# A reordered opening, weight-major FFN for the first batch, and moved masks in a fused attention and FFN kernel

## The chip, the core and the metric

The kernel runs on one core of one Trainium2 chip. The core has five engines that run side by side, each with its own instruction queue that it works through in order: TensorE (PE in the profile, matrix products), VectorE (DVE), ScalarE (ACT, which has the exponential), GpSimd (POOL) and SyncE (SP, which only issues transfers here). Sixteen DMA engines move data between the chip's main memory and the core's own memory. Matrix products land in a small accumulator memory, PSUM. An engine waits for another through semaphores.

The metric is the device time of one execution in microseconds (us), as the median of five runs.

## What is computed

There are 4 batches, 8 heads, 768 positions and 64 numbers per head. Some heads look at the whole past, the others only at the first 4 positions and the last 64. Behind the attention stands a feed-forward network (FFN) with three weights whose products are combined by maximum.

```python
scores = scale * np.matmul(q, k.transpose(0, 1, 3, 2))
causal = rel >= 0
stream_keep = causal & (is_sink | in_win)
mask = np.where(retr[0, :, 0, 0, None, None], full_mask, stream_mask)
...
a = np.exp(scores)
a = a / (np.sum(a, axis=-1, keepdims=True) + 1e-09)
return np.matmul(a, v)
...
h = np.maximum(np.maximum(x @ w1, x @ w2), x @ w3)
return h @ w_out
```

Inputs and output are 32-bit floats; the kernel computes in 16-bit floats with 32-bit sums.

## The kernel before

**Tiling.** Work is cut into steps `t` of one batch `b`, one half of the 768 positions as queries and one quad of four heads; sixteen steps, t = 0 to 15, with t = 0 and 1 the first half of batch 0, t = 2 and 3 its second half, t = 4 to 7 batch 1. A step has two pairs of heads, `i` = 0 and 1, and its scores come in units `u`: two for a first half, four for a second.

**A step.** `scores` (line 439) makes one unit's products of keys and queries in PSUM; ACT takes the exponential into `pt` (line 450). For t = 0 and 1 the mask is added inside PSUM by a product with `ident` (line 423), which needs the mask tile `mk` of those heads; for later steps the exponential is multiplied by the mask (line 477), on POOL unless `(t, i, u)` stands in `MASK_ON_DVE`. `prep_v` casts the values into `va` (line 390) and makes `vf` (line 392), which is zero for far keys in heads that don't look far. `av` (line 493) multiplies `pt` with `va` and `vf`; DVE divides by the sum (lines 501 and 503) into `x`. The transposed `x`, `xT`, is made by a DMA transpose for most steps, and by PE with a copy (lines 525 and 529, `turn_x`) for t = 0, 1 and 3.

**FFN.** When the second quad of a half is done, `ffn(b, half)` is put in a queue. It is a generator of 24 pieces: 18 groups of four products (line 336), one for each of three weights and six column blocks, and then three output rows of six products (line 362), counted as two pieces each. The group of the first weight is cast to `acc` by ACT (line 344); those of the other two are combined by maximum on DVE (line 347), the last into `hT`. `fill(n)` takes n pieces from the queue. A group holds one of four PSUM banks until its cast or maximum is done. The groups go column block by column block, three weights each, except for the first FFN, where all of the first weight comes first.

**Order.** The order on every engine is the order of the program text; nothing is rearranged. The opening, from line 537 to 592, is written out by hand. From then on `PROGRAM` (line 600) has one row for each unit of scores from t = 2: how many FFN pieces belong to it, whether its two pairs are to be apart, and four lines of other work that go between the scores and the fills: `v` (prep_v with its engines, as d, a, p), `av`, `x` (turn_x), `turn` (a DVE transpose of keys or queries, line 188), `pair` (turn_pair), `cast`, `load`, `load_v` and `gate`, which makes SP wait for an exponential before it loads further values.

**Keys and queries.** Those of batch 0 are loaded as 32-bit floats in pairs of heads (`load_pairs`), cast to 16 bits (`cast_pair`, line 137), transposed by PE and copied out as `KQ` (`turn_pair`, lines 155 and 160). In the opening, pairs 0 to 3 of the first half come by SP's and ACT's queues. Later ones, and the four weights (`load_weight`, lines 305 and 310), are issued from POOL's queue.

**Flags.** `read_flags` reads which heads look far, `head_flags` spreads this over the partitions by a product, `head_masks` makes the mask tile of two heads (line 293), and `far_flags` makes the tile `far` on DVE and copies it into `vf` on POOL (line 288). `idle_work` issues products that nobody reads.

Of the kernel before, what the change touches and what calls it, by code (L numbers as in the profile page):

```python
# [49 lines left out]
def kernel(  # L50
# [14 lines left out]
    nc = tc.nc  # L65
# [50 lines left out]
    cast = {}  # L116
# [151 lines left out]
    def read_flags():  # L268
        nc.vector.tensor_scalar(
            out=RT1, in0=ir32[:, 0 : 2 * H : 2], scalar1=0.0, scalar2=None,  # L270
            op0=ALU.not_equal,
        )

    def head_flags():
        flags = bank([P, H], FP32, "flags")
        nc.tensor.matmul(flags, base[0:1, 0:P], RT1, start=True, stop=True)
        nc.vector.tensor_copy(out=RT, in_=flags)
        nc.vector.tensor_scalar(
            out=least, in0=RT, scalar1=-1.0, scalar2=1.5, op0=ALU.mult, op1=ALU.add
        )  # L280
# [36 lines left out]
    def ffn(b, half):  # L317
        last = b == B - 1 and half == 1
        n_yy = 0

        def psum():
            nonlocal n_yy
            n_yy += 1
            if last and n_yy % 2:
                return sps.tile([P, 2, 512], FP32, tag="st", name="yst")[:, 0, :]
            return bank([P, 512], FP32, "yy")

        hT = [htp.tile([P, HALF], FP16, tag=f"hT{n}", name=f"hT{n}") for n in range(NNB)]
        acc = {}
        order = [(wi, ni) for ni in range(NNB) for wi in range(3)]  # L330
        if (b, half) == (0, 0):
            order.sort()
        for wi, ni in order:
            yy = psum()
            for ks in range(KS):
                nc.tensor.matmul(  # L336
                    yy[:, 0:HALF],
                    w_t[wi][:, ks, ni * P : (ni + 1) * P],
                    xT[b, half][ks].rearrange("p a t -> p (a t)"),
                    start=(ks == 0), stop=(ks == KS - 1),  # L340
                )
            if wi == 0:
                acc[ni] = accp.tile([P, HALF], FP16, tag="acc", name="acc")
                nc.scalar.copy(out=acc[ni], in_=yy[:, 0:HALF])  # L344
            else:
                dst = acc[ni] if wi == 1 else hT[ni]
                nc.vector.tensor_tensor(  # L347
                    out=dst, in0=yy[:, 0:HALF], in1=acc[ni], op=ALU.max
                )
            yield  # L350
        for tb in range(HB):

            parts = 2 if last and tb == HB - 1 else 1
            n = DMdl // parts
            r0 = b * S + half * HALF + tb * P
            ot = fwork.tile([P, DMdl], FP32, tag="ot", name="ot")
            for c, op, eng in (
                (0, nc.scalar.copy, nc.sync), (n, nc.vector.tensor_copy, nc.scalar),
            )[:parts]:
                yo = psum()  # L360
                for ns in range(NNB):
                    nc.tensor.matmul(  # L362
                        yo[:, 0:n],
                        hT[ns][:, tb * P : (tb + 1) * P],
                        woutt[:, ns, c : c + n],
                        start=(ns == 0), stop=(ns == NNB - 1),
                    )
                op(out=ot[:, c : c + n], in_=yo[:, 0:n])  # L368
                eng.dma_start(out=out[r0 : r0 + P, c : c + n], in_=ot[:, c : c + n])
            yield  # L370
            yield
# [83 lines left out]
                masks(t, i, u)  # L455


    MASK_ON_DVE = ((3, 1, 3), (6, 0, 1), (7, 0, 1))

    def masks(t, i, u):  # L460
        b, half, qd = where(t)
# [56 lines left out]
    def turn_x(t, i, op=None):  # L518
# [17 lines left out]
    dve, act, pool = nc.vector.tensor_copy, nc.scalar.copy, nc.gpsimd.tensor_copy  # L536
    idle_work(8)
    cast_pair(0, 0, (act, act))
    read_flags()
    head_flags()  # L540
    head_masks(0, True)
    turn_pair(0, 0, dve, dve)
    idle_work(2)
    cast_pair(0, 1, (pool, act))
    head_masks(1, True)
    turn_pair(0, 1, dve)
    cast_pair(0, 2, (pool, pool))
    scores(0, 0, (0,))
    turn_pair(0, 2, dve)
    scores(0, 0, (1,))  # L550
    head_masks(2, True)
    head_masks(3, True)
    cast_pair(0, 3, (pool, pool))
    scores(0, 1, (0,))
    load_weight(0)
    turn_pair(0, 3, dve)
    far_flags()
    prep_v(0, 0, dve, nc.gpsimd)
    scores(0, 1, (1,))
    prep_v(0, 1, dve, nc.vector)  # L560
    prep_v(1, 0, dve, nc.vector)
    scores(1, 0, (0,))
    scores(1, 1, (0,))
    prep_v(1, 1, dve, nc.gpsimd)
    load_pairs(1, 0, 2, (nc.gpsimd, nc.gpsimd))
    scores(1, 0, (1,))
    scores(1, 1, (1,))
    av(0, 0)
    load_weight(1)
    av(0, 1)  # L570
    load_pairs(1, 2, 2, (nc.gpsimd, nc.gpsimd))
    av(1, 0)
    turn_x(0, 0, act)
    turn_x(0, 1, act)
    av(1, 1)
    turn_x(1, 0, act)
    load_weight(2)
    load_v(0, 1, (nc.gpsimd,) * HB)
    load_weight(3)
    turn_x(1, 1, dve)  # L580
    cast_pair(1, 0, (dve, act))
    cast_pair(1, 1, (dve, act))
    fill(4)
    turn_pair(1, 0, dve)
    turn_pair(1, 1, dve)
    head_masks(0)
    head_masks(1)
    fill(1)
    head_masks(2)
    fill(1)  # L590
    fill(1)
    head_masks(3)

# [2 lines left out]

    FIRST = 4
    PROGRAM = (  # L600
        (2.4, True, "", "", "cast 1 2 dd", "cast 1 3 ap"),
        (2.4, False, "load 1 0", "", "", ""),
        (2.0, False, "pair 1 2", "", "", "pair 1 3"),
        (2.2, False, "load 1 1", "", "", ""),
        (2.2, True, "", "", "v 2 0 dd", "gate"),
        (1.6, True, "v 2 1 ap, load_v 1 0", "", "av 2 0", ""),
        (1.6, True, "", "x 2 0, turn 1 0 0 0, turn 1 0 0 1", "av 2 1, turn 1 0 1 1", "v 3 0 pp"),
        (3.0, False, "turn 1 0 1 0, load_v 1 1", "x 2 1", "", "v 3 1 ap"),
        (3.6, False, "", "turn 1 1 0 0, turn 1 1 0 1, turn 1 1 1 1, av 3 0", "", "v 4 0 pd"),
        (3.0, False, "av 3 1", "", "", "turn 1 1 1 0, v 4 1 ad"),  # L610
        (3.6, False, "x 3 0, x 3 1", "", "av 4 0", ""),
        (3.6, False, "", "v 5 0 ad, x 4 0, av 4 1", "", "v 5 1 ap, load 2 0"),
        (2.8, False, "", "x 4 1", "", ""),
        (3.6, False, "av 5 0, av 5 1, load 2 1", "x 5 0", "", ""),
        (3.8, False, "v 6 0 pp", "x 5 1", "", "load_v 2 0"),
        (3.4, False, "", "v 6 1 dp", "", "turn 2 0 1 0"),
        (4.8, False, "", "turn 2 0 0 1", "av 6 0", "turn 2 0 0 0"),
        (4.0, False, "", "", "x 6 0, turn 2 0 1 1", "x 6 1"),
        (3.4, False, "", "av 6 1", "turn 2 1 0 0, turn 2 1 0 1", "load_v 2 1"),
        (5.0, False, "", "v 7 0 dp", "turn 2 1 1 0, turn 2 1 1 1", ""),  # L620
        (4.0, False, "v 7 1 dp", "", "", "v 8 0 ap"),
        (3.6, False, "av 7 0, x 7 0, av 7 1", "", "", "v 8 1 dp"),
        (4.0, False, "", "v 9 0 dp", "av 8 0, x 7 1", ""),
        (4.0, False, "", "av 8 1", "x 8 0", "load 3 0"),
        (4.0, False, "", "x 8 1", "av 9 0, v 9 1 dp", ""),
        (4.0, False, "load 3 1", "", "x 9 0", ""),
        (4.2, False, "v 10 0 dp, av 9 1", "", "x 9 1", "load_v 3 0"),
        (4.0, False, "v 10 1 dp", "", "", "turn 3 0 1 0"),
        (4.0, False, "", "turn 3 0 0 1, av 10 0", "", "x 10 0, turn 3 0 0 0"),
        (4.0, False, "", "", "av 10 1, turn 3 0 1 1", ""),  # L630
        (4.4, False, "", "x 10 1", "turn 3 1 0 0, turn 3 1 0 1", "v 11 0 dp, load_v 3 1"),
        (3.2, False, "", "", "turn 3 1 1 0, turn 3 1 1 1", "v 11 1 dp"),
        (4.0, False, "", "", "av 11 0", "v 12 0 dp"),
        (4.2, False, "x 11 0, av 11 1", "", "", "v 12 1 dp"),
        (4.8, False, "", "v 13 0 dp, x 11 1", "av 12 0", ""),
        (4.0, False, "", "av 12 1", "x 12 0", ""),
        (3.2, False, "", "x 12 1", "av 13 0, v 13 1 dp", ""),
        (4.0, False, "", "", "x 13 0", ""),
        (4.0, False, "v 14 0 dp, av 13 1", "", "x 13 1", ""),
        (4.0, False, "v 14 1 dp", "", "", ""),  # L640
        (4.0, False, "", "av 14 0", "", "x 14 0"),
        (4.0, False, "", "", "av 14 1", ""),
        (4.0, False, "", "x 14 1", "", "v 15 0 pp"),
        (4.2, False, "", "", "", "v 15 1 dp"),
        (4.0, False, "", "", "av 15 0", ""),
        (4.0, False, "x 15 0, av 15 1", "", "", ""),
        (4.0, False, "", "x 15 1", "", ""),
    )
    ops = {"d": dve, "a": act, "p": pool}
    engines = {"d": nc.vector, "p": nc.gpsimd}  # L650
# [2 lines left out]
        av=lambda *a: av(*map(int, a)),  # L653
# [71 lines left out]
```

## Time and profile before

| what | value |
| --- | --- |
| median of 5 runs | 203.6 us (203.57 to 203.91) |
| the profiled execution, device time | 204.2 us |
| its span in the trace | 202.2 us |
| PE busy | 190.0 us, 94% of the span |
| DVE busy | 130.2 us, 64% |
| POOL busy | 125.5 us, 62% |
| ACT busy | 124.8 us, 62% |
| granted PE clock, mean | 0.997 |
| transfers | 26.48 MB, mean 131 GB/s |

The span runs from the first to the last instruction that the trace shows; the device time includes what lies around it. All times inside the trace count from the span's start. A row of the profile that names a group, such as `L336 PE MATMUL yy<-xT,w1t`, gives the line, the engine, the operation, and what it writes and reads. The idle time of an engine is put down to the one that it waited for last. The DMA share is the busy share of the sixteen DMA engines, and can pass 1 when their packets overlap.

### The profile page before, as it was taken

What the parts mean: (1) busy time and instruction counts of PE and PEld (TensorE: products, weight loads), DVE (VectorE), ACT (ScalarE), POOL (GpSimd) and SP (SyncE); (2) the same over time, 40 slices, a digit from 0 to 9 for tenths busy, and PEclk for the clock granted to TensorE, in tenths of its full rate; (3) what the DMA queues carried; (4) which work ended last, traced back from release to release, by engine and by line L of the source; (5) the groups of instructions that cost most, each with busy time, mean ns of one, the idle gap of its engine ahead of it and who ended that gap; (6) DMA issues with size and microseconds to landing.
All of it is one profiled execution on the core that took longest, in us unless ns stands there. A gap on an engine that the chain in (4) does not pass through costs nothing.

```text
span 202.2 us, 5148 instructions
## 1 busy us (share of the span) xinstructions
PE 190.0 (94%) x2059; PEld 108.6 (54%) x2059; DVE 130.2 (64%) x260; ACT 124.8 (62%) x188; POOL 125.5 (62%) x151
## 2 busy tenths in 40 slices
PE   7897599996799999999999999999999999999992
PEld 2454355545456456565556466574565565655552
DVE  2995698689666766985565748986647244633540
ACT  4493687887577778565758596656586776323221
POOL 3659349879996933859987906798929636700000
PEclk9999999999999999999999999999999999999998
DMA  6999999996938996532449983613301230014004
GB/s 187 267 153 225 250 246 211 214 217 144 216 102 141 198 211 138 122 56 74 145 78 204 181 199 87 138 21 124 93 19 24 83 95 19 3 41 154 3 0 156
DMA packets 43245, 26.48 MB, mean 131 GB/s; under 512 B 33558, under 2 KB 38230, under 8 KB 43222
## 3 DMA queue, kind: packets, MB, share of 16 engines
q1 hardware_dynamic: 37206, 15.01, 32.4%
q0 software_dynamic: 4784, 10.23, 26.1%
q10 hardware_dynamic: 1232, 0.92, 1.5%
q8 instruction: 16, 0.26, 0.6%
q14 instruction: 7, 0.06, 0.1%
HBM read 25.17 MB, written 6.29 MB: 156 GB/s over the span
## 4 chain that ended last, share of the span: by engine, by line
PE 78%; POOL 6%; DMA 6%; DVE 5%; ACT 2%; issue 2%; DVEq 0%; ACTq 0%
PE yy L336 41%; PE yy L362 13%; PE st L439 9%; PE oacc L493 9%; DMA w1t<-in_moe_w_dram 5%; POOL pt L477 4%; PE yst L336 3%; PE st L226 2%; DVE KQ L160 2%; DVE mk L293 1%; POOL vf L392 1%; ACT pt L450 1%; DMA out_dram<-ot 1%; PE yst L362 1%; ACT ot L368 1%
## 5 line engine op out<-in xcount | busy, mean ns | idle before, releaser
L477 POOL TENSOR_TENSOR pt<-pt,mk 128x512 f16<-128x512 f16 (+1 forms) x81 | 86.6, 1093 | 31.4 <-ACT pt L450 31.4
L450 ACT ACTIVATE pt<-st 128x1024 f16<-128x1024 f32 (+3 forms) x99 | 83.0, 894 | 26.3 <-PE st L439 25.5
L347 DVE TENSOR_TENSOR acc<-yy,acc 128x384 f16<-128x384 f32 x45 | 25.1, 559 | 25.8 <-PE yy L336 17.9
L336 PE MATMUL yy<-xT,w1t 128*128 128x384 f16 x180 | 36.5, 327 | 0.4 <-DMA w1t<-in_moe_w_dram 0.4
L336 PE MATMUL yy<-xT,w2t 128*128 128x384 f16 x180 | 36.3, 327 | 0.0
L336 PE MATMUL yy<-xT,w0t 128*128 128x384 f16 x180 | 36.1, 326 | 0.1
L344 ACT CAST acc<-yy 128x384 f16<-128x384 f32 x45 | 21.3, 481 | 19.9 <-PE yy L336 14.9
L362 PE MATMUL yy<-woutt,hT 128*128 128x512 f16 (+1 forms) x138 | 32.3, 375 | 0.0
L439 PE MATMUL st<-KQ 32*128 32x384 f16 (+5 forms) x560 | 28.5, 279 | 1.9 <-DVE KQ L188 1.2
L347 DVE TENSOR_TENSOR hT<-yy,acc 128x384 f16<-128x384 f32 x45 | 25.1, 557 | 6.4 <-PE yy L336 3.2
L493 PEld LDWEIGHTS <-pt 128*128 128x128 f16 x672 | 23.8, 97 | 5.3 <-issue 1.4
L188 DVE STREAM_TRANSPOSE KQ<-kq 128x384 f32<-128x384 f32 x24 | 25.2, 1137 | 1.0 <-DMA kq<-in_k_dram 1.0
L493 PE MATMUL oacc<-va,pt 128*128 128x65 f16 x352 | 24.8, 193 | 0.7 <-POOL pt L477 0.6
L336 PEld LDWEIGHTS <-w2t 128*128 128x128 f16 x192 | 17.6, 98 | 13.0 <-issue 1.9
L336 PEld LDWEIGHTS <-w0t 128*128 128x128 f16 x192 | 17.8, 97 | 12.2 <-issue 0.9
L336 PEld LDWEIGHTS <-w1t 128*128 128x128 f16 x192 | 17.3, 98 | 12.8 <-issue 1.0
L439 PEld LDWEIGHTS <-KQ 32*128 32x128 f16 (+1 forms) x560 | 12.2, 93 | 20.1 <-issue 13.1
L368 ACT COPY ot<-yy 128x512 f32<-128x512 f32 x22 | 12.9, 588 | 14.9 <-PE yy L362 10.7
L362 PEld LDWEIGHTS <-hT 128*128 128x128 f16 x150 | 13.9, 98 | 15.1 <-DVE hT L347 0.9
L493 PE MATMUL oacc<-vf,pt 128*128 128x65 f16 x320 | 21.3, 193 | 0.2 <-DVE vf L392 0.2
L503 DVE TENSOR_TENSOR x<-oacc,rc 128x384 f16<-128x384 f32 x32 | 17.8, 558 | 1.1
L501 DVE RECIPROCAL rc<-oacc 128x6 f32<-128x6 f32 x32 | 6.2, 193 | 18.6 <-PE oacc L493 18.3
(71 smaller groups left out, 125.3 us busy)
## 6 DMA issues: line engine op xcount, KB each, us to landing
out_dram<-ot SPq DMA_DIRECT2D x23, 256.0 KB, 2.7
vs<-in_v_dram SPq DMA_DIRECT2D x21, 256.0 KB, 5.3
kq<-in_k_dram POOLq DMA_DIRECT2D x6, 384.0 KB, 7.9
kq<-in_q_dram POOLq DMA_DIRECT2D x6, 384.0 KB, 9.5
qs<-in_q_dram ACTq DMA_DIRECT2D x4, 192.0 KB, 4.0
ks<-in_k_dram SPq DMA_DIRECT2D x4, 192.0 KB, 3.9
w0t<-in_moe_w_dram POOLq DMA_DIRECT2D x1, 768.0 KB, 7.1
ks<-in_k_dram POOLq DMA_DIRECT2D x2, 384.0 KB, 8.1
```

Of the source, the lines that this page charges most:

```text
L188: nc.vector.transpose(out=dst.rearrange("c (p j) -> c j p", j=n)[:, j0:j1], in_=src.rearrange("c (j i) -> c j i", i=R),)
L336: nc.tensor.matmul(yy[:, 0:HALF], w_t[wi][:, ks, ni * P : (ni + 1) * P], xT[b, half][ks].rearrange("p a t -> p (a t)"), start=(ks == 0), s ...
L344: nc.scalar.copy(out=acc[ni], in_=yy[:, 0:HALF])
L347: nc.vector.tensor_tensor(out=dst, in0=yy[:, 0:HALF], in1=acc[ni], op=ALU.max)
L362: nc.tensor.matmul(yo[:, 0:n], hT[ns][:, tb * P : (tb + 1) * P], woutt[:, ns, c : c + n], start=(ns == 0), stop=(ns == NNB - 1),)
L368: op(out=ot[:, c : c + n], in_=yo[:, 0:n])
L439: nc.tensor.matmul(sts[g // m][:, g % m, c0 : c0 + n * P], KQ[rows, 0, ki * P : (ki + 1) * P], KQ[rows, 1, t0 : t0 + n * P], start=(c0 == ...
L450: nc.scalar.activation(out=pts[t, i][:, u, h0 : h0 + m, 0:w], in_=st[:, :, 0:w], func=AF.Exp, scale=sc,)
L477: engine.tensor_tensor(out=x, in0=x, in1=m, op=ALU.mult)
L493: nc.tensor.matmul(o[:, qi, hl, 0 : D + 1], pt[:, u, hl, c : c + P], vv[:, 2 * hp + hl, ki, 0 : D + 1], start=(idx == 0), stop=(idx == len ...
L501: nc.vector.reciprocal(out=rc, in_=o[:, :, :, D])
L503: nc.vector.tensor_tensor(out=x, in0=o[:, :, :, 0:D], in1=rc.unsqueeze(3).to_broadcast([P, HB, 2, D]), op=ALU.mult,)
```

## The change

It does five things.

1. In the opening, the two idle products come ahead of the flags instead of after pair 0; masks are made after the pair 0 copies; the scores of pairs 0 and 1 come ahead of the casts and turns of pairs 2 and 3; the load of the first weight and the far flags stand between the casts of pair 2 and pair 3.
2. Behind that, the value preparations and `av` steps are in another order, one value cast goes from DVE to POOL, and the casts and masks for the second half are distributed differently.
3. The FFNs of both halves of batch 0 go by weight, not only the first.
4. Seven instead of three masks are listed for DVE: (2,0,1), (3,0,1), (5,0,0), (5,0,1) and (5,1,0) are added and (6,0,1) goes back to POOL.
5. `PROGRAM` has other numbers of pieces and other places for most of its work.

```diff
         acc = {}
         order = [(wi, ni) for ni in range(NNB) for wi in range(3)]
-        if (b, half) == (0, 0):
+        if b == 0:
             order.sort()
...
-    MASK_ON_DVE = ((3, 1, 3), (6, 0, 1), (7, 0, 1))
+    MASK_ON_DVE = ((2, 0, 1), (3, 0, 1), (3, 1, 3), (5, 0, 0), (5, 0, 1), (5, 1, 0), (7, 0, 1))
...
     idle_work(8)
     cast_pair(0, 0, (act, act))
     read_flags()
+    idle_work(2)
     head_flags()
+    turn_pair(0, 0, dve, dve)
     head_masks(0, True)
-    turn_pair(0, 0, dve, dve)
-    idle_work(2)
     cast_pair(0, 1, (pool, act))
     head_masks(1, True)
     turn_pair(0, 1, dve)
+    scores(0, 0, (0,))
     cast_pair(0, 2, (pool, pool))
-    scores(0, 0, (0,))
-    turn_pair(0, 2, dve)
+    scores(0, 1, (0,))
+    load_weight(0)
+    far_flags()
     scores(0, 0, (1,))
     head_masks(2, True)
     head_masks(3, True)
     cast_pair(0, 3, (pool, pool))
-    scores(0, 1, (0,))
-    load_weight(0)
+    turn_pair(0, 2, dve)
+    scores(0, 1, (1,))
     turn_pair(0, 3, dve)
-    far_flags()
     prep_v(0, 0, dve, nc.gpsimd)
-    scores(0, 1, (1,))
-    prep_v(0, 1, dve, nc.vector)
     prep_v(1, 0, dve, nc.vector)
+    load_pairs(1, 0, 2, (nc.gpsimd, nc.gpsimd))
     scores(1, 0, (0,))
     scores(1, 1, (0,))
-    prep_v(1, 1, dve, nc.gpsimd)
-    load_pairs(1, 0, 2, (nc.gpsimd, nc.gpsimd))
     scores(1, 0, (1,))
+    prep_v(1, 1, pool, nc.gpsimd)
+    load_weight(1)
+    prep_v(0, 1, dve, nc.vector)
+    av(0, 0)
     scores(1, 1, (1,))
-    av(0, 0)
-    load_weight(1)
+    av(1, 0)
     av(0, 1)
     load_pairs(1, 2, 2, (nc.gpsimd, nc.gpsimd))
-    av(1, 0)
     turn_x(0, 0, act)
+    av(1, 1)
     turn_x(0, 1, act)
-    av(1, 1)
-    turn_x(1, 0, act)
+    cast_pair(1, 1, (act, act))
+    head_masks(0)
     load_weight(2)
     load_v(0, 1, (nc.gpsimd,) * HB)
+    turn_x(1, 0, dve)
+    turn_x(1, 1, dve)
+    cast_pair(1, 0, (act, dve))
+    fill(4)
+    head_masks(2)
     load_weight(3)
-    turn_x(1, 1, dve)
-    cast_pair(1, 0, (dve, act))
-    cast_pair(1, 1, (dve, act))
-    fill(4)
+    turn_pair(1, 1, dve)
     turn_pair(1, 0, dve)
-    turn_pair(1, 1, dve)
-    head_masks(0)
     head_masks(1)
-    fill(1)
-    head_masks(2)
+    head_masks(3)
     fill(1)
     fill(1)
-    head_masks(3)
+    fill(1)
...
     PROGRAM = (
-        (2.4, True, "", "", "cast 1 2 dd", "cast 1 3 ap"),
-        (2.4, False, "load 1 0", "", "", ""),
-        (2.0, False, "pair 1 2", "", "", "pair 1 3"),
-        (2.2, False, "load 1 1", "", "", ""),
-        (2.2, True, "", "", "v 2 0 dd", "gate"),
-        (1.6, True, "v 2 1 ap, load_v 1 0", "", "av 2 0", ""),
-        (1.6, True, "", "x 2 0, turn 1 0 0 0, turn 1 0 0 1", "av 2 1, turn 1 0 1 1", "v 3 0 pp"),
-        (3.0, False, "turn 1 0 1 0, load_v 1 1", "x 2 1", "", "v 3 1 ap"),
-        (3.6, False, "", "turn 1 1 0 0, turn 1 1 0 1, turn 1 1 1 1, av 3 0", "", "v 4 0 pd"),
-        (3.0, False, "av 3 1", "", "", "turn 1 1 1 0, v 4 1 ad"),
-        (3.6, False, "x 3 0, x 3 1", "", "av 4 0", ""),
-        (3.6, False, "", "v 5 0 ad, x 4 0, av 4 1", "", "v 5 1 ap, load 2 0"),
+        (2.4, True, "", "cast 1 2 dp", "", ""),
+        (2.4, True, "load 1 0, cast 1 3 dp", "", "", ""),
+        (2.0, False, "pair 1 2", "", "", "load 1 1"),
+        (2.2, False, "pair 1 3", "v 2 0 dd", "", ""),
+        (2.2, True, "", "gate", "v 2 1 ap", "load_v 1 0"),
+        (1.6, False, "", "av 2 0", "", "turn 1 0 0 0"),
+        (1.6, True, "", "turn 1 0 0 1", "av 2 1, load_v 1 1", "turn 1 0 1 1"),
+        (2.2, False, "turn 1 0 1 0", "v 3 0 ap", "x 2 0", "v 3 1 pp"),
+        (3.6, False, "turn 1 1 0 1", "x 2 1, turn 1 1 0 0, turn 1 1 1 1, av 3 0", "", ""),
+        (2.8, False, "v 4 0 pp, av 3 1", "", "turn 1 1 1 0", "v 4 1 ad"),
+        (3.6, False, "x 3 0, x 3 1", "", "", "av 4 0"),
+        (3.6, False, "", "", "x 4 0, v 5 1 pp", "av 4 1, x 4 1, v 5 0 ad"),
...
     )
```

## The prediction

> **What bounds the kernel now.** I read the page's first table, then the busy time by stage, the chain of waits, the transfers, and last the opening instruction by instruction. TensorE (PE) is busy 190.0 of 202.2 us, so 12.2 us are open. The stage table says where (columns: PE, weight loads, VectorE (DVE), ScalarE (ACT), GpSimd (POOL), then granted clock, DMA share, GB/s):
>
> ```profile
> 0.00:7.00 7.00, 5.74 (x27) 2.58 (x27) 3.30 (x14) 2.71 (x5) 2.25 (x10) 1.00 0.75 226
> 7.00:18.00 11.00, 8.99 (x120) 5.36 (x119) 10.02 (x26) 7.67 (x14) 8.64 (x15) 1.00 1.08 196
> 18.00:25.00 7.00, 5.04 (x38) 2.91 (x35) 3.42 (x7) 3.25 (x8) 3.85 (x5) 1.00 1.04 237
> 25.00:39.00 14.00, 13.48 (x127) 7.45 (x128) 12.10 (x26) 11.20 (x15) 10.43 (x13) 1.00 1.14 225
> 39.00:46.00 7.00, 6.52 (x77) 3.17 (x77) 5.51 (x9) 5.50 (x8) 5.73 (x7) 1.00 1.05 216
> 46.00:52.40 6.40, 4.31 (x106) 3.02 (x106) 6.31 (x13) 3.98 (x7) 6.40 (x9) 1.00 0.60 150
> 52.40:70.00 17.60, 17.50 (x197) 9.99 (x189) 11.02 (x25) 13.62 (x20) 15.62 (x19) 1.00 0.81 160
> ```
>
> Of PE's idle time 1.3 us lie before its first matmul, 4.0 in 7 to 25, 0.5 in 25 to 39, 0.5 in 39 to 46, 2.1 in 46 to 52.4, 0.2 in all of 52.4 to 183, and 3.6 in the end, whose PE order the change leaves alone. Only the first 52 us can give anything, 7 us at most; after that PE is full, and a gain or loss made by 52 us is carried to the end unless the new order opens holes. The chain of waits through the opening (start, length, what):
>
> ```profile
> 14.62 0.74 POOL qs L124
> 15.36 9.66 DMA w1t<-in_moe_w_dram
> 25.02 0.05 issue
> 25.06 0.82 PE yy L336 x4
> ```
>
> The reader is to see that the first FFN waits for its second weight, w1: its issue stands in POOL's queue at 15.36, and it lands at 25.02. It is not alone: the stages from 7 to 46 have a DMA share above 1.0, and POOL's loads follow one another. So I ask where the DMA was *not* full:
>
> ```profile
> 10.00:11.00 1.00, 0.70 (x10) 0.45 (x8) 1.00 (x6) 1.00 (x3) 0.08 (x1) 1.00 0.89 112
> 11.00:12.00 1.00, 1.00 (x9) 0.52 (x10) 1.00 (x3) 0.71 (x3) 0.00 (x0) 1.00 0.88 43
> 16.00:17.00 1.00, 0.87 (x18) 0.79 (x18) 0.82 (x4) 0.77 (x2) 1.00 (x3) 1.00 0.64 175
> 17.00:18.00 1.00, 0.41 (x7) 0.25 (x5) 0.66 (x2) 0.48 (x1) 1.00 (x2) 1.00 1.09 363
> ```
>
> At 10 to 12 only 43 to 112 GB/s move, because w0, issued at 9.14, has hardly begun (it lands 7.1 us after its issue, 16.2). At 16 to 17 there is a second dip: w0 is in, and the pair load behind it was issued only at 13.81.
>
> **The change, part by part.** I follow each engine's new order with the old durations.
>
> *Flags and pair 0.* The two idle matmuls now precede the flags matmul. Ten start 0.44 apart (before, eight took 1.26 to 4.79), so flags come at 5.67 (+0.88), `least` is done at 6.27, and the two KQ copies of pair 0 (0.93) end at 7.20, against 7.26, as the masks no longer precede them. But masks 0 and 1 now follow, beside POOL's casts of pair 2.
>
> What such neighbours cost is the first unknown:
>
> ```profile
> 7.19 1.10 DVE L293 TENSOR_SCALAR mk<-kept,least 128x512 f16<-128x512 f16 x2
> 7.13 0.51 POOL L137 CAST kn<-ks 128x384 f16<-128x384 f32 x1 [1.21 <-DMA ks<-in_k_dram]
> 9.94 1.12 DVE L293 TENSOR_SCALAR mk<-kept,least 128x512 f16<-128x512 f16 x4
> ```
>
> A mask takes 0.28 with POOL quiet (four in 1.12) and 0.55 beside POOL's casts (two in 1.10). So masks 0 and 1 end at 8.30, and the first exponential comes 1.0 later, at 8.75. Masks 2, 3 (0.56), KQ pair 1 (0.87) and the far flags (0.25) end at 9.98. Masks 4 to 7 stand beside four POOL operations (two far copies, casts of pair 3): between 1.12 (quiet) and 2.3 (0.58 for each mask with its POOL operation); I take 2.2, as the rows with a busy POOL are the nearer. KQ pairs 2 and 3 (1.73) then end at 13.9; before, 11.93.
>
> *To the first FFN.* DVE's v casts took 12.17 to 14.28; one (0.35) goes to POOL, so 1.75, to 15.65. Four reciprocal-and-multiply steps, 0.70 apart: 18.45. Masks of pair 0 for later, moved in front: 0.56. Two xT copies, 0.36 each: 19.75. Before, the last xT was done at 18.49. **The opening's compute is thus 1.25 later**, and this costs nothing only because of what it waited for: w0's 24 matmuls at 0.1625 and 12 transposes (0.66), with three matmuls ahead of the last xT, end at 23.9, and w1 was not there until 25.02. ACT's casts of the next pairs held its first `acc` until 21.89, which held PE's banks; three casts now end 1.0 after that pair load lands, about 21.2, and PE's first four groups end at 21.9, so this wait goes.
>
> *POOL's queue.* Casts of pair 2 end at 8.14; w0 is issued at 8.2 (−0.94), past pair 3's casts. POOL then waits for `far` (9.98); behind it stand the two copies, pair 3's casts (2.2 together, to 12.2), one vf (0.45), the pair loads (0.81 and 0.77, from 12.65 against 13.81), the va cast and vf (0.95), and w1, at 15.2 against 15.36. Who waits for pair 3 is DVE's copy at 13.0, after it.
>
> Here a rule speaks against the change. The Trainium skill ("SBUF — State Buffer", "A bandwidth-pool intuition that's wrong") says that GpSimd's descriptor writing is shut out while VectorE holds the shared port in a two-port mode: a load of 620 ns took 3100. The new place of w0's issue is beside masks 2 and 3, which by the mask rows contend with POOL; the old was beside a KQ copy, which kept 0.86 with and without POOL. The row of the issue is 0.94 (w1 0.78). By the rule's ratio it takes 4.7, POOL's queue slips 3.8, and w1 lands some 3 us late; by the trace only two masks of 0.28 can hold the port, so 0.94 to 1.5. I take 1.0; the later `far` wait swallows it.
>
> *The transfers.* w0 fills the dip at 10 to 12 and may land 0.94 earlier; the pair loads, issued 1.16 earlier, close the dip at 16. w1's own issue is only 0.16 earlier, but the stream ahead is what it queued behind. Its landing moves by between 0 (the DMA is full anyway) and 1.1; I take **0.8: 24.2**, later than w0's end at 23.9. First w1 matmul: 24.25 instead of 25.06.
>
> *25 to 46.* PE's order is nearly the old one. Eight masks stood at 24.7 to 27.3 on DVE; four now come earlier (about 1.1 freed), and mask (2,0,1) comes over from POOL (0.57): cover remains. v(2,0) is prepared a row earlier, which removes up to 0.38 (holes at 37.9 and 38.3). I count none of it: w_out is issued at 21.26, needs 18.0, lands at 39.26, and is used at 39.30. PE cannot get there faster than the stream. The same holds for kq, for which DVE waits until 41.19. So −0.8 stays −0.8.
>
> *46 to 52.4.* PE's order is identical. DVE is busy 6.31 of 6.40 and POOL all of it. SP's queue there changes in one place: the second v load of batch 1 moves ahead of an output store, which nobody waits for. DVE loses one vf (0.28); mask (3,0,1) leaves POOL (1.1), but POOL idled 1.19 before 42.38 for an exponential, so that buys nothing directly; mask (3,0,3) now precedes two v steps. POOL gets v(4,0)'s steps (about 1.0), after the masks that PE needs. Taken: −0.2; bounds 0 to −0.7.
>
> *FFN of (0,1) by weight.* ACT gets six `acc` casts (0.48) within six groups instead of two. ACT in that stretch: exponentials 1.94 + 1.09, casts 2.9, one va 0.5, together 6.4 us, against PE's 6×0.65 + 0.9 scores + 0.9 of av = 5.7. The excess of 0.7 is mostly taken up by four banks. DVE, free of maxima then, takes the five masks of t=5 (about 2.6), and afterwards has 12 maxima (6.7) and three x steps (2.3) in 11 us: it fits. Cost 0 to 0.7; taken 0.1. The later rows move va casts from DVE to POOL and ACT; PE's holes there are 0.2 in all, so nothing.
>
> **Sum**: −0.8 −0.2 +0.1 = **−0.9**: the profiled execution's 204.2 would be 203.3. It stands 0.6 over the median of 203.6, so the forecast is 202.7.
>
> **Rivals.** What a measurement can tell from no change is 0.2%, 0.4 us.
>
> *The stream does not move* (0.17): the share is 1.39 at 8 to 10, where w0 would now start, so it only displaces v's packets; w1's own issue is earlier by 0.16. Against it: the two dips. Result −0.2: 203.4.
>
> *Both holes close* (0.11): the stream gains 1.1 and the 46 to 52 stage 0.7: 201.8.
>
> *POOL's queue blocks* (0.21): VectorE's masks and POOL's operations hold each other up everywhere, `far` is late, and pair 3, the pair loads and w1 all stand behind it. For it: the mask rows, the rule above, and that the sum leaves w1 a lead of 0.16 only. Against: the stream has slack to absorb about 0.9. It decides when w1 is issued after 16.3 or the last xT copy is after 20.9; each microsecond beyond is one on the end. With w0's issue stretched by 1.5 and each later neighbour at the long price (another 0.4), w1 is issued at 17.1: +0.8, 204.4.
>
> *Forecast as summed* (0.51): 202.2 to 203.2.
>
> **Chances**: faster 0.62 (0.51 + 0.11), within 0.17, slower 0.21. The range, 201.5 to 204.5, takes in both outer rivals' centres.
>
> **What would show it.** Right: w0's issue near 8.2, first exponential near 8.75, last xT copy near 19.75 and yet first w1 matmul near 24.2; 46 to 52.4 with the same holes, shifted. Wrong: w1 issued after 16.3; masks 4 to 7 over 2.3; holes of more than 0.5 us between 52 and 70, with ACT full.

## The result, and the profile after

| kernel | median, us | lowest to highest | executions |
| --- | --- | --- | --- |
| before | 203.64 | 202.25 to 205.59 | 76 |
| after | 204.11 | 202.04 to 206.36 | 41 |

The ratio after/before is 0.9994, with an interval from 0.9976 to 1.0013: no difference that this measurement can tell. The ratio leaves out slow executions, those more than 1.5% above the fastest of their kernel (8 of the 41 after), while the medians in the table take in all. The forecast was 202.7, faster. The execution that was profiled took 202.6, with a span of 200.7, so the trace below belongs to an execution 1.5 under the median. Why that is so is part of the result.

The stages of the changed kernel, from 18 us on (start and end, length, then busy time and number of instructions of PE, weight loads, DVE, ACT and POOL, then granted clock, DMA share, GB/s):

```profile
18.00:25.00 7.00, 6.61 (x53) 3.97 (x52) 5.38 (x14) 4.47 (x10) 2.58 (x4) 1.00 1.12 258
25.00:39.00 14.00, 11.65 (x120) 6.42 (x118) 12.41 (x19) 10.10 (x12) 9.79 (x12) 1.00 1.13 220
39.00:46.00 7.00, 6.86 (x77) 3.17 (x75) 6.38 (x11) 5.93 (x10) 5.01 (x5) 1.00 0.98 198
46.00:52.40 6.40, 4.38 (x93) 3.14 (x93) 5.95 (x11) 3.71 (x6) 6.32 (x10) 1.00 0.94 235
52.40:70.00 17.60, 17.60 (x205) 10.22 (x203) 14.15 (x29) 13.04 (x20) 14.02 (x17) 1.00 0.69 109
```

From 18 to 25 PE now works for 6.61 us where it had 5.04: the opening's hole in front of w1 is gone. From 25 to 39 it works for 11.65 of 14 where it had 13.48: a hole of the same size has opened where the prediction said "cover remains". The two stages behind it are about as before, and 52.4 to 70 is full. The chain of waits (start, length, what) names the instruction that made the new hole:

```profile
18.86 12.55 DMA vs<-in_v_dram
31.42 0.55 issue
31.97 3.35 DVE va L390
35.33 0.02 issue
35.35 0.56 DVE vf L392
35.91 0.48 DVE hT L347
36.38 0.04 issue
36.43 0.81 PE yy L336 x4
```

The last part of the values, issued at 18.86, landed 13.0 us later, at 31.90 (31.42, where the chain ends that step, is the end of DVE's copy before it). DVE started to cast them at 31.97, and this one cast (line 390, v(2,0)) lasted 3.34 us. Its product `vf` and a maximum follow, and only then PE's next group. The same place in order of time, DVE, POOL and PE (start, length, engine and line, operation, out<-in, shape, count, and in brackets the idle time before it with what ended it):

```profile
31.68 0.59 POOL L172 DMA_DIRECT2D kq<-in_k_dram  x1
31.97 3.34 DVE L390 CAST va<-vs 128x384 f16<-128x384 f32 x1 [0.55 <-issue]
32.27 0.54 POOL L172 DMA_DIRECT2D kq<-in_q_dram  x1
...
32.81 2.27 POOL L477 TENSOR_TENSOR pt<-pt,mk 128x512 f16<-128x512 f16 x2
...
35.83 2.40 DVE L347 TENSOR_TENSOR hT<-yy,acc 128x384 f16<-128x384 f32 x5
...
36.43 0.81 PE L336 MATMUL yy<-xT,w2t 128*128 128x384 f16 x4 [2.35 <-DVE hT L347]
```

The reader is to see three things. DVE is busy, not waiting, for 3.34 us with an operation that takes 0.34 to 0.83 in its fifteen other instances. POOL works without a gap from 31.68 to 35.08, with two load issues and two masks, and the cast ends 0.23 after the last mask. And five maxima (0.48 each) stand in a row behind the cast: with all four PSUM banks unread, PE waits 2.35 us.

The list of all instances of that line (duration in ns as least, median and most) shows how far out it is:

```profile
L390 DVE CAST va<-vs x16: 335/561/3342, 12.5 to 155.1; 128x384 f16<-128x384 f32 x16
```

So a gain in the opening was paid for by one instruction at 32 us. What was left to find: whether the cast was held by POOL, what the rest of the change is worth without it, and why a kernel whose trace shows 200.7 has a median over that of the old.

### The profile page after: what moved, and what is told of

It is laid out like the page before. It is cut to its first block, busy times and chain, and to the rows that moved or that the text cites. A ratio compares the mean times of both kernels' runs of the same rounds, so it can differ in the third digit from the quotient of the medians.

```text
span 200.7 us, 5127 instructions
## 1 busy us (share of the span) xinstructions
PE 188.7 (94%) x2059; PEld 109.4 (55%) x2059; DVE 131.3 (65%) x259; ACT 125.0 (62%) x189; POOL 122.5 (61%) x151
## 4 chain that ended last, share of the span: by engine, by line
PE 75%; DMA 10%; DVE 5%; POOL 5%; ACT 1%; issue 1%; SPq 1%; POOLq 0%; ACTq 0%
PE yy L336 40%; PE yy L362 13%; PE st L439 9%; PE oacc L493 9%; DMA vs<-in_v_dram 6%; PE yst L336 3%; DMA ks<-in_k_dram 3%; DVE KQ L188 2%; DVE va L390 2%; DMA out_dram<-ot 1%; POOL vs L206 1%; POOL qs L124 1%; ACT pt L450 1%; PE yst L362 1%; ACT ot L368 1%
## 5 line engine op out<-in xcount | busy, mean ns | idle before, releaser
L477 POOL TENSOR_TENSOR pt<-pt,mk 128x512 f16<-128x512 f16 (+1 forms) x75 | 80.7, 1098 | 37.2 <-ACT pt L450 37.1
L336 PE MATMUL yy<-xT,w0t 128*128 128x384 f16 x180 | 35.6, 326 | 0.4 <-DVE xT L529 0.4
L439 PE MATMUL st<-KQ 32*128 32x384 f16 (+4 forms) x560 | 28.6, 279 | 0.7 <-DVE KQ L188 0.7
L188 DVE STREAM_TRANSPOSE KQ<-kq 128x384 f32<-128x384 f32 x24 | 25.8, 1128 | 0.0
L336 PEld LDWEIGHTS <-w2t 128*128 128x128 f16 x192 | 17.1, 98 | 15.7 <-issue 4.7
```

The source lines that it names most:

```text
L188: nc.vector.transpose(out=dst.rearrange("c (p j) -> c j p", j=n)[:, j0:j1], in_=src.rearrange("c (j i) -> c j i", i=R),)
L336: nc.tensor.matmul(yy[:, 0:HALF], w_t[wi][:, ks, ni * P : (ni + 1) * P], xT[b, half][ks].rearrange("p a t -> p (a t)"), start=(ks == 0), s ...
L439: nc.tensor.matmul(sts[g // m][:, g % m, c0 : c0 + n * P], KQ[rows, 0, ki * P : (ki + 1) * P], KQ[rows, 1, t0 : t0 + n * P], start=(c0 == ...
L477: engine.tensor_tensor(out=x, in0=x, in1=m, op=ALU.mult)
```

## The experiments

Three theories stood at the start, by the names that the expectations give them. **Port**: v(2,0)'s cast at its new place is held by POOL's unbroken run, because the two engines share something that only one can use, and the hole eats what the opening gained. **Transfer**: values and keys land when they land, so that a gain in the opening only moves a hole. **Later stages**: the FFN by weight and the moved masks lose what the opening gains. All ratios below are to the kernel before; medians are of 22 executions where this is said, else of 6.

### The two halves of the change alone

`open_only` is the old kernel with the new opening, up to the first row of `PROGRAM`. `rest_only` is the new kernel with the old opening.

> The kernel before with the new opening alone (rows, masks and FFN order are the old ones, so v(2,0) has its old place). Port theory: first w1 product near 22.8 as in the changed kernel, no block at v(2,0), 0.988 to 0.995. Transfer theory: first w1 near 22.8, all given back by 46, 0.998 to 1.000. Later-stages theory: 0.992 to 0.996, since the loss lies in what this kernel leaves out.

> The changed kernel with the old opening (new rows, masks and FFN order). Port theory: w1 at 25.1 as before, and v(2,0)'s cast again beside POOL's run, a hole of 1 to 2.5 us near 36: 1.004 to 1.010. Transfer theory: 1.000. Later-stages theory: 1.003 to 1.006, with holes after 52 and none at 36.

| kernel | median, us | ratio | interval |
| --- | --- | --- | --- |
| open_only (22 executions) | 203.3 | 0.9965 | 0.9939 to 0.9991 |
| rest_only (22 executions) | 205.19 | 1.0068 | 1.0041 to 1.0094 |

The opening gives 0.35%, 0.7 us: what the prediction counted for it. Its 0.9965 lies in none of the three expected ranges, so it doesn't decide between them. The rest costs 0.68%, 1.4 us, as the port theory had it. `rest_only` has the long cast too, 33.31 to 35.93, again beside two masks that end at 35.71, and PE waits 2.36 behind it. The loss comes with the rest, whatever the opening.

### The cast moved, and given to another engine

`v20_late` moves the one step a row later, behind the masks; `v20_ap` leaves it where it is, but has ACT cast and POOL multiply.

```diff
-        (2.2, False, "pair 1 3", "v 2 0 dd", "", ""),
-        (2.2, True, "", "gate", "v 2 1 ap", "load_v 1 0"),
+        (2.2, False, "pair 1 3", "", "", ""),
+        (2.2, True, "", "gate", "v 2 0 dd, v 2 1 ap", "load_v 1 0"),
```

```diff
-        (2.2, False, "pair 1 3", "v 2 0 dd", "", ""),
+        (2.2, False, "pair 1 3", "v 2 0 ap", "", ""),
```

> The changed kernel with one edit: VectorE's value cast and product of v(2,0) stand a row later, behind the gate, about where the kernel before had them. Port theory (the cast, 3.34 us instead of 0.35, is held off by POOL's unbroken run of two load issues and two masks, and the FFN's maxima wait behind it): the 2.35 us hole of TensorE at 34 to 36 goes or falls under 0.5, the first output product comes near 37, and the time falls by 1.0 to 2.0 us against the changed kernel, to 0.990 to 0.995 of the kernel before. Transfer theory (values and keys land when they land, so a hole only moves): the hole moves behind the new place or to 45 to 52, time within 0.3 us of the kernel before. Later-stages theory (the FFN by weight and the moved masks lose what the opening gains): no change, same as the kernel before.

> The changed kernel with one edit: v(2,0)'s cast goes to ScalarE and its product to POOL, at the same place. Port theory: VectorE isn't touched, so the maxima run on; hole at 34 to 36 gone, 0.990 to 0.995 of the kernel before, unless the product on POOL, now behind the two masks, makes av(2,0) wait (at most 0.5). Transfer theory: ScalarE waits for the values in VectorE's place and the hole stays. Later-stages theory: same as the kernel before.

`v20_late` took 201.44, ratio 0.9865 (0.982 to 0.991). `v20_ap` took 201.51, ratio 0.9882 (0.9841 to 0.9923). Both are faster than both kernels, and by more than the 0.990 to 0.995 that the port theory had expected; where the rest comes from is told under the clock. In the order of time, `v20_late` has:

```profile
34.04 2.28 POOL L477 TENSOR_TENSOR pt<-pt,mk 128x512 f16<-128x512 f16 x2
...
34.48 1.47 PE L336 MATMUL yy<-xT,w2t 128*128 128x384 f16 x8
35.34 0.56 DVE L347 TENSOR_TENSOR hT<-yy,acc 128x384 f16<-128x384 f32 x1 [0.74 <-PE yy L336]
35.82 0.72 DVE L390 CAST va<-vs 128x384 f16<-128x384 f32 x1
```

The maxima come ahead of the cast, PE's groups run on without a wait, and the cast, which now meets only the end of the second mask (36.32), takes 0.72. Its stages from 18 to 52.4 answer to those shown of the changed kernel:

```profile
18.00:25.00 7.00, 6.24 (x49) 3.65 (x51) 5.57 (x14) 4.26 (x10) 3.32 (x4) 1.00 1.08 230
25.00:39.00 14.00, 13.62 (x135) 7.43 (x130) 11.81 (x22) 11.61 (x13) 10.12 (x13) 1.00 1.14 223
39.00:46.00 7.00, 6.26 (x74) 2.93 (x73) 6.21 (x9) 5.97 (x9) 5.26 (x6) 1.00 1.00 205
46.00:52.40 6.40, 4.94 (x97) 3.46 (x97) 5.38 (x11) 3.70 (x7) 6.32 (x9) 1.00 0.73 167
```

From 25 to 39 PE works for 13.62 us instead of 11.65. Some of that is given back from 39 to 46 (6.26 instead of 6.86); over the four stages it is 31.06 against 29.50, so 1.56 us more in these two executions.

One step of one head group, moved by one row, is worth 1.3%. Both versions take DVE's cast away from that place, so they don't yet say what held it there.

### The same move made in the old kernel

```diff
-        (2.2, False, "load 1 1", "", "", ""),
-        (2.2, True, "", "", "v 2 0 dd", "gate"),
+        (2.2, False, "load 1 1", "v 2 0 dd", "", ""),
+        (2.2, True, "", "", "", "gate"),
```

> The kernel before; only v(2,0) moves one row earlier, as the change did. Port theory: the cast lands beside POOL's load issues and masks, takes 2 to 3 us, and the FFN's last maxima and TensorE wait: 1.004 to 1.010, most of what the new rows with the old opening lost (1.0068). If the loss of those rows lies elsewhere: 0.999 to 1.001.

It took 206.1, ratio 1.0098 (1.0067 to 1.013). The move alone, with nothing else of the change, costs 1%.

```profile
34.74 2.29 POOL L477 TENSOR_TENSOR pt<-pt,mk 128x512 f16<-128x512 f16 x2
...
35.39 1.86 DVE L390 CAST va<-vs 128x384 f16<-128x384 f32 x1 [2.05 <-DMA vs<-in_v_dram]
...
38.37 0.81 PE L336 MATMUL yy<-xT,w2t 128*128 128x384 f16 x4 [2.37 <-DVE hT L347]
```

Here the cast starts while the first mask runs (34.74 to about 35.89), and the second mask still goes ahead of it. It ends at 37.25, 0.22 after POOL's 37.03. Its 1.86 us are less than the 2 to 3 expected, since part of this hole is the values themselves: DVE waited for them until 35.39. In the changed kernel they were there at 31.90.

### POOL moved instead of DVE

If POOL's run holds the cast, the cast may stay and POOL's work may go. `after_load_late` issues the two loads of keys and queries a row later, behind the masks; DVE's order is untouched.

```diff
-        (2.0, False, "pair 1 2", "", "", "load 1 1"),
-        (2.2, False, "pair 1 3", "v 2 0 dd", "", ""),
+        (2.0, False, "pair 1 2", "", "", ""),
+        (2.2, False, "pair 1 3", "v 2 0 dd, load 1 1", "", ""),
```

> The changed kernel; VectorE's order is untouched, and v(2,0)'s cast keeps its early place. Only POOL's two load issues for t=6 and 7 move behind its two masks of (2,.,3), so POOL has nothing to run between 31.7 and 32.8. Port theory: a cast that starts in that gap takes 0.35 to 0.7 us instead of 3.34, the hole at 34 to 36 goes, 0.987 to 0.992 of the kernel before; one that starts after the first mask is held until the second ends (2.5). Late-values theory (the cast's length is a wait for the values): the cast ends at 35.3 again, hole and time as in the changed kernel, 0.998 to 1.000.

It took 202.24, ratio 0.9906 (0.9878 to 0.9934).

```profile
30.14 4.91 POOL L477 TENSOR_TENSOR pt<-pt,mk 128x512 f16<-128x512 f16 x4 [0.26 <-ACT pt L450]
...
32.25 0.37 DVE L390 CAST va<-vs 128x384 f16<-128x384 f32 x1 [0.17 <-issue]
32.65 1.39 DVE L392 TENSOR_TENSOR vf<-va,far 128x384 f16<-128x384 f16 x1
...
33.92 1.48 PE L336 MATMUL yy<-xT,w2t 128*128 128x384 f16 x8
```

The cast starts 0.28 us later than in the changed kernel and takes 0.37 instead of 3.34. The gap in POOL's work that had been expected did not come; the cast ran across the border of two masks (32.40), and this time POOL paid: four masks take 4.91, where two elsewhere take 2.27, so 0.37 more than twice that. The product behind it, which reads two tensors, was held past the end of the next mask (33.63, the product to 34.04; 1.39 instead of 0.56), and PE has no wait. This settles the cause: with the same DVE order, and the values landed less than 0.1 us before the start in both, the cast is long or short by what POOL is doing. It does not show what decides who goes first. In the changed kernel the cast stood ready 0.84 us before the first mask began and still waited for both.

### Only the product on DVE

`v20_ad` leaves the cast to ACT and the product to DVE at the early place.

```diff
-        (2.2, False, "pair 1 3", "v 2 0 dd", "", ""),
+        (2.2, False, "pair 1 3", "v 2 0 ad", "", ""),
```

> One look. The changed kernel with v(2,0)'s cast on ScalarE and its product (two inputs in the core's memory) still on VectorE at the early place. If the block hits only the cast: the product takes 0.56 to 0.7, hole gone. If it hits the product too: it takes 1.4 to 2.5, ending about 0.2 after one of POOL's two masks, hole of 0.5 to 1.5.

One execution: 202.75, with a span of 200.8.

```profile
33.04 2.96 DVE L392 TENSOR_TENSOR vf<-va,far 128x384 f16<-128x384 f16 x1 [1.13 <-ACT va L390]
...
33.30 2.27 POOL L477 TENSOR_TENSOR pt<-pt,mk 128x512 f16<-128x512 f16 x2
```

The two-input product is held in the same way, from 33.04 to 36.0, 0.43 after the masks end and longer than the 1.4 to 2.5 expected, and PE's wait for `hT` is 1.95. So it isn't the cast alone that is bad at this place: both DVE operations that were tried there were held.

### What the other parts are worth

With the cast out of the way, parts of the change can be undone one by one from `v20_late`: the FFN order of the second half, the list of masks, the place of w0's load; and `late_both` has `v20_late`'s and `after_load_late`'s moves together.

```diff
-        if b == 0:
+        if (b, half) == (0, 0):
```

> The version with v(2,0) a row later (0.9865) and the FFN of the second half of batch 0 back to column block by column block. If going by weight pays: 0.990 to 0.993. If it costs what the prediction had (0.1 us) or nothing: 0.986 to 0.987. If it costs up to 0.7: 0.983.

```diff
-    MASK_ON_DVE = ((2, 0, 1), (3, 0, 1), (3, 1, 3), (5, 0, 0), (5, 0, 1), (5, 1, 0), (7, 0, 1))
+    MASK_ON_DVE = ((3, 1, 3), (6, 0, 1), (7, 0, 1))
```

> The version with v(2,0) a row later (0.9865) and the old three masks on VectorE. If the moved masks pay, POOL being full from 46 to 60: 0.990 to 0.993, with TensorE's holes from 46 to 56 longer by 0.5 to 1.3. If they don't matter, as the prediction had it: 0.986 to 0.988.

```diff
-    load_weight(0)
-    far_flags()
...
     cast_pair(0, 3, (pool, pool))
+    load_weight(0)
+    far_flags()
```

> The version with v(2,0) a row later (0.9865), with the load of w0 and the far flags put back behind the casts of pair 3, as the kernel before had them on POOL's queue; the rest of the new opening stays. If the early w0 carries the opening's gain, as the prediction had it: 0.989 to 0.992, w1's landing 0.5 to 1.0 us later. If the transfers are full anyway, or the gain comes from the pair loads and casts behind: 0.986 to 0.988.

> The version with v(2,0) a row later (0.9865), and POOL's two load issues for t=6 and 7 a row later as well. Port theory: the cast has lost its block already, so nothing more is to be had: 0.985 to 0.989. If POOL's issues hold up VectorE in other places too: 0.980 to 0.984.

| kernel | median, us | ratio | interval |
| --- | --- | --- | --- |
| v20_late | 201.44 | 0.9865 | 0.982 to 0.991 |
| with the old FFN order | 202.11 | 0.9918 | 0.9891 to 0.9944 |
| with the old masks (22 executions) | 203.64 | 0.9985 | 0.9963 to 1.0008 |
| with w0's old place | 201.6 | 0.989 | 0.985 to 0.9929 |
| with the loads a row later too | 201.47 | 0.9885 | 0.9849 to 0.9921 |

**The masks** are the one clear part: without their new places the whole gain is gone. The busy time of one window, first with the old masks, then `v20_late` (columns as in the stage table):

```profile
53.00:70.00 17.00, 16.99 (x200) 9.77 (x198) 11.78 (x25) 12.22 (x19) 16.57 (x21) 1.00 0.72 134
```

```profile
53.00:70.00 17.00, 17.00 (x200) 9.77 (x198) 14.11 (x29) 12.40 (x20) 13.41 (x17) 1.00 0.83 151
```

PE is full in both; POOL has 16.57 of 17 us in the first and 13.41 in the second. The price comes later, as the list of PE's waits (total, times, longest), the order of time and the chain of waits of the kernel with the old masks show:

```profile
PE yy L336 <- DMA xT<-x: 2.0, 1, 2.0
```

```profile
75.26 0.32 PE L336 MATMUL yy<-xT,w0t 128*128 128x384 f16 x1 [2.02 <-DMA xT<-x]
```

```profile
64.99 10.23 DMA xT<-x
75.22 0.04 issue
```

The next FFN stands for 2.02 us at its transposed `x`; in the trace of `v20_late` that wait is not there. The `x` itself was hardly late: it was done at 64.96, against 64.02 in `v20_late` and 64.58 in the changed kernel, where PE doesn't wait here either. But its DMA transpose took 10.2 us to land. What a full POOL does show beside it is that the loads of keys and queries for batch 2, issued at 57.55 and 58.13 in `v20_late`, left POOL's queue only at 60.80 and 61.38, with the next two at 64.61 and 65.20, so that all four were under way with the transpose. That they held it is likely and not shown. Nor need the wait be as long in other executions, since this one took 205.04, 1.4 over its kernel's median. What had been expected was 0.990 to 0.993, by longer holes between 46 and 56. **FFN by weight**: undone, PE waits 0.49 us at 54.25 for a maximum (`acc`, line 347), which fits a gain of half a microsecond; but the intervals of the two ratios touch, so its size is not settled. **w0's place** is inconclusive: the intervals overlap almost wholly. **The loads later too** bring nothing beyond `v20_late`: the two moves remove the same hole.

### Where the rest of the loss was: the clock

By the stages above, `v20_late` gains 1.56 us on the changed kernel from 18 to 52.4, and the two profiled spans differ by only 0.6 (200.7 and 200.1), yet the medians differ by 2.7 (204.11 and 201.44). The missing part is in the granted clock. `before_v20_early`, microsecond by microsecond around its hole (the number before the DMA share is the clock):

```profile
37.00:38.00 1.00, 0.00 (x0) 0.00 (x0) 0.97 (x3) 0.47 (x2) 0.48 (x2) 1.00 1.08 208
38.00:39.00 1.00, 0.63 (x4) 0.29 (x3) 1.00 (x3) 0.00 (x0) 0.53 (x1) 1.00 1.09 212
39.00:40.00 1.00, 1.00 (x13) 0.42 (x12) 1.00 (x3) 0.45 (x1) 0.00 (x0) 0.70 1.09 215
40.00:41.00 1.00, 1.00 (x22) 1.00 (x20) 0.17 (x1) 1.00 (x2) 0.35 (x1) 0.50 1.09 212
41.00:42.00 1.00, 1.00 (x15) 0.72 (x13) 0.24 (x2) 0.48 (x1) 1.00 (x2) 0.50 1.07 207
42.00:43.00 1.00, 1.00 (x4) 0.34 (x3) 1.00 (x2) 0.00 (x0) 0.91 (x1) 0.60 1.08 215
```

The hole ends at 38.37, and from about 39.4 to 42.8 PE runs at half clock: 0.30 + 0.50 + 0.50 + 0.40 = 1.7 us of work lost, though PE counts as busy. `rest_only` shows the same 0.70, 0.50, 0.50, 0.60 behind its hole (38 to 42), and `open_only` 0.75, 0.50, 0.50, 0.55 (50 to 54) behind three waits between 47.9 and 50.1 (0.27, 0.56 and 0.69 us), which the kernel before has as well. One such drop makes the mean clock of an execution 1 − 1.7/205 = 0.992, so executions can be sorted by their mean clock, at least 0.996 or at most 0.992:

| kernel | at 0.996 or more | at 0.992 or less |
| --- | --- | --- |
| before (43 executions) | 32: 203.5 us | 11: 205.05 us |
| after (41) | 19: 202.85 us | 22: 204.9 us |
| open_only (22) | 12: 202.25 us | 10: 203.75 us |
| rest_only (22) | 8: 204.72 us | 14: 205.64 us |
| before_v20_early (6) | 1: 205.26 us | 5: 206.33 us |
| v20_late (6) | 6: 201.44 us | none |

Before drops in 26% of its executions, after in 54%, `v20_late` in none of six. The hole thus costs twice: 202.85 − 201.44 = 1.4 us at full clock, and a drop of about 2 us in every second execution. The profiled execution of the changed kernel had the hole and kept its clock at 1.00 through it: the trace showed the first price and not the second. That this hole brings the drop is supported by the drop's place right behind it in two traces, and by its going with the hole: of the 63 executions of the changed kernel and `rest_only`, 36 are at 0.992 or less; of the 58 of the seven kernels with the new rows and without the hole, 4. It is not the only place for a drop, as `open_only` shows, and what decides in which execution one comes is open.

## Why the prediction was wrong

**The opening: right in size, in part by luck.** It counted −0.8 (w1 later in the sum than w0's end, first product at 24.25); `open_only` measured −0.7, with an interval from −1.2 to −0.2. At full clock it gives more, 203.5 to 202.25, and its clock drops (10 of 22 executions, against 11 of 43) take part of that back; no drop was in the sum. The steps were mostly early: first exponential at 8.05 (8.75 forecast), w1's issue at 14.02 (15.2), last xT copy done at 18.62 (19.75), w1's first product at 22.75. Four masks beside POOL took 1.39 and 1.60, where 2.2 was put for the second four. The 2.3 us between 25.06 and 22.75 are not all the change's: with the old opening, `rest_only` has this product at 23.35 and `before_v20_early` at 24.6.

**The rule that was weighed, and where.** The prediction set the rule of the shared port from the Trainium skill ("SBUF — State Buffer", "A bandwidth-pool intuition that's wrong") against w0's issue, which by an estimate from that rule was to grow from 0.94 to 4.7; it took 0.94. In this trace it stood beside a copy of keys (DVE 7.95 to 8.89), not beside masks; in `v20_late` it stood wholly beside masks (DVE 7.57 to 8.99) and took 0.93. The row was right there. The rule was then laid aside for the rest of the change, and in its mirror image it decided the result: not POOL held by DVE, but DVE by POOL.

**The step that failed** is in *25 to 46*: "cover remains. v(2,0) is prepared a row earlier, which removes up to 0.38 [...] I count none of it." It was counted as at worst nothing. The runs showed a cast held for 3.34 us, 1.4 us at full clock and a clock drop in half of the executions besides: 0.9994 against 0.9865 without it, about 1.3% or 2.6 us. The step was costed by PE's order and by what it no longer waits for. What stood on the *other* engine at the new place was left out, although the trace before had it:

```profile
34.05 0.59 POOL L172 DMA_DIRECT2D kq<-in_k_dram  x1
...
34.64 0.54 POOL L172 DMA_DIRECT2D kq<-in_q_dram  x1
...
35.18 2.28 POOL L477 TENSOR_TENSOR pt<-pt,mk 128x512 f16<-128x512 f16 x2
...
36.96 0.72 DVE L390 CAST va<-vs 128x384 f16<-128x384 f32 x1
```

There the same cast stood beside the last of two masks that follow two load issues without a gap (34.05 to 37.46), and took 0.72. A row earlier meant the front of that run instead of its tail. And what stood behind it on DVE, the maxima that empty PE's banks, was not named.

**The rival "POOL's queue blocks"** had the right pair of engines, and that they hold each other up, but the wrong place, and only POOL's lateness in its sum: it looked at the opening, with POOL late for w1. "Holes of more than 0.5 us between 52 and 70" did not come; the hole was at 34 to 36, where no sign had been asked for.

**46 to 52.4**: PE stands idle for 2.02 of 6.40 us, against 2.09, so of the −0.2 there is 0.07. The holes are not the same ones: the wait of 0.57 for a mask is gone and those for `x` fell from 0.82 to 0.35, but two for `vf` from POOL (0.73 and 0.26) are new.

**The masks were mis-sized.** "That buys nothing directly" and a share of −0.2 stood for them; undoing them costs 0.9985 against 0.9865, 1.2%, and the one trace has a wait of 2.02 us at 73 to 75, where the prediction put nothing. That holds for the new rows of `PROGRAM`; with the old rows, where PE was idle for 0.2 us from 52.4 to 183, the old masks did no such harm. **FFN by weight** was put at +0.1; the runs lean to about −0.5 (201.44 against 201.9 without it, at full clock), unsettled.

So the forecast had gains too small and one loss missing, and the two cancelled in the median.

## What to carry to other kernels

Before a DVE cast or two-input product is moved, read what POOL does at the new place, not only which operands are ready: beside a run of POOL work without a gap, price it, at worst, at the whole rest of that run, and then ask which operations stand behind it on DVE and what they set free. A held operation appears in a trace as one long busy instruction, so compare least, median and most duration of a line. A new hole of over 2 us in PE should be priced with the clock drop that may follow it, and a single trace may not show that drop: sort the executions by mean granted clock.

## What the runs showed of the hardware

- **A waiting DVE operation is passed over more than once.** The Trainium skill ("SBUF — State Buffer", "Who interferes with whom") says that VectorE and GpSimd share a port pair that one of them holds for a whole instruction, the other being shut out, by order of issue. The traces agree on the block (0.34 to 3.34 us), but it did not end with the instruction that was running: in the changed kernel the cast started beside the first of two issues and waited through two masks; in `before_v20_early` it started in the first mask, and the second still went ahead. In both, as in `rest_only`, `v20_late` and the kernel before, it ended 0.22 to 0.23 us after the last mask. In `after_load_late` it got in at the border of two masks. In these five traces two load issues stand ahead of the two masks; in `after_load_late` none does. Whether that decides it is open.
- **What of a load's issue holds a cast is open**, too: in `late_both` the cast ran in 0.35 us (35.56 to 35.91) wholly beside an issue (35.46 to 36.02), with no mask behind it.
- **A hole of 2.4 us can be enough for the clock to fall.** The skill ("TensorE: Matmul & The Clock Gate", "Part 1: The HAM clock gate") gives an idle window of about 3.4 us before the clock halves, in windows that run freely. Here holes of 2.36 and 2.37 us were followed by half clock, while the profiled execution of the changed kernel kept its clock behind 2.35 us. The half clock's length, 3.4 us, is that of the window.
